# First chunk of a long convolution in two causal halves of 256 rows, so that the first FFN unit follows the first half

## The chip, the cores and the metric

One Trainium2 chip, one of its cores. The metric is the device time of one execution in microseconds, a median over executions. A profile adds the span, which is 1.7 to 1.8 us shorter than the time of the same execution (before: the profiled execution took 358.32 us, span 356.5).

## The reference, cut to what matters

Two layers, each a gated long convolution followed by a gated FFN, on 2048 rows of width 512 (FFN width 1792):

```python
def _A_ref(q, k, v, shift_k, ssm_k, ssm_D):
    k_shift = sum over t in 0..3 of k_pad[:, t:t+S, :] * shift_k[:, 3-t]   # cut: a loop
    kv = k_shift * v
    y = irfft(rfft(kv padded to 2S) * rfft(ssm_k padded to 2S))[:S]        # cut: causal convolution
    y = y + kv * ssm_D
    return q * y
def _B_ref(x, w_gate, w_up, w_down):
    return (silu(x @ w_gate) * (x @ w_up)) @ w_down

x = A_q
x = x + _A_ref(_layernorm(x), A_k, A_v, A_shift_k, A_ssm_k, A_ssm_D)
x = x + _B_ref(_layernorm(x), B_w_gate, B_w_up, B_w_down)
# and the same two lines once more
```

k, v, ssm_k are the same in both layers, so the convolution result y is computed once.

## The kernel before

The rows go in four chunks of 512. A chunk's y comes from products of spectra X (of k_shift * v) and G (of the filter h = ssm_k, D added to its row 0), each a 1024-point transform made by TensorE matmuls with tables `fwd` and `inv`, ScalarE evictions and VectorE butterflies. The FFN runs in 16 units of 256 rows (layer, chunk, half). A planner in the kernel's own Python gives each operation a cost and each transfer a latency (`lat`), and from these it works out one fixed order for each engine. TensorE, VectorE, ScalarE and the queue on SP each work through their order. Where the planner sees the head idle, it puts dummy matmuls (`wm`) to hold the clock.

The head, in program order (cut):

```python
transpose_k(0, "pf", ("ACT", "DVE"))               # k of chunk 0, 16 TensorE transposes
hs = transpose_h(0, "pf", (2, 0, 1, 3), False, ("ACT", "DVE"))
shift_mul(0, "pf", False)                          # 64 matmuls, then times v
normed[0, 0, 0] = apply_norm(0, 0)
...
for par in (0, 1):
    half(hs, ev, par, 2.0 / N, "pf", ("ACT", "ACT"), False)   # transform of h, 512 rows
    butterfly(ev, G[0], par, False)
...
direct(vt[0], X[0], "pf", ("ACT", "ACT"))          # transform of k_shift*v, 512 rows
for slot in (0, 2, 1, 3):
    product(0, 0, [slot], False)
...
inverse_direct(0, (0, 2, 1, 3))
first = prologue(0, 0, 0, True)                    # y -> x -> statistics -> z -> zT
prologue(0, 0, 1)
...
conv(1)
for c in range(NB):
    run((0, c, 0)); run((0, c, 1))                 # FFN units
    ...
```

The constants at the top say which engine does which statistics (`ST1`, `ST2`), normalisations (`Z_ACT`, `N_ACT`), h transposes (`H_DMA`) and residual adds (`X_PE`, an add by an identity matmul), and with how much slack the planner works (`SLK`, `ASL`, `HSL`). They were searched for this kernel.

## Time and profile before

| | before |
|---|---|
| time, median of 2 runs | 357.74 us (357.62 to 357.85) |
| span of the profiled run | 356.5 us |
| first FFN matmul | 37.09 us |
| TensorE work ahead of it, without dummies | 28.1 us |
| last matmul ends | 353.19 us |
| VectorE, ScalarE busy | 281.1, 238.0 us |

How to read it: split the span at the first FFN matmul and at the end of the last matmul. Ahead of the first cut TensorE has 28.1 us of work and 9.0 us without. Between the cuts lie 316.1 us; the counted work there is 342.5 - 28.1 = 314.4, so 1.7 us are waits. After the last matmul come 3.3 us. The 28.1 us are TensorE's busy time from 7.07 to 37.09; the count by pitch gives 27.8, so head idle and waits of the kernel before are good to some 0.3 us. And its profiled execution (358.32 us) is among the slowest on record for it: the run "fewer dummies in the kernel before" below has the same head and tail in an execution of 357.67 us, and its middle is 315.5 us, 0.6 less. So 1.1 us of waits are usual. I use the same four terms (head idle, waits in the middle, tail, work) for every kernel below, with work otherwise counted by matmuls and their pitch (the time from the start of one to the start of the next) and not by busy time.

### The profile page before, as it was taken

To read this page: it belongs to the slowest core of one execution; us is meant where nothing else is said; L and a number is where in the kernel's file an instruction comes from. 1 tells how busy PE (TensorE), PEld (TensorE's weight loads), DVE (VectorE), ACT (ScalarE), POOL (GpSimd) and SP (SyncE) were. 2 spreads that over 40 slices of the span, in tenths; PEclk is the share of its full clock that TensorE was granted. 3 is DMA by queue.
4 is the path that set the end of the run, shared out by engine and by line. 5 is a ranking of instruction groups with operands and counts; after the bars stand their busy time and mean duration, and the time that the engine had idled before them with its cause. 6 is when DMAs were issued, how large, how long until landed. Compare 5 with 4: busy or idle time off the path is not lost.

```text
span 356.5 us, 6735 instructions
## 1 busy us (share of the span) xinstructions
PE 347.6 (97%) x2689; PEld 254.4 (71%) x2712; DVE 281.1 (79%) x517; ACT 238.0 (67%) x454; POOL 39.3 (11%) x42
## 2 busy tenths in 40 slices
PE   7999999999999999999999999999999999999996
PEld 6655985867778585868668685858686777768673
DVE  6997999999989999999999999889985323626020
ACT  4587693838878493648878994848484775647352
POOL 1010010130320200111121000201101000101000
PEclk9999999999999999999999999999999999999999
DMA  7999021010241341010311042010103020101000
GB/s 263 306 353 293 2 69 22 0 31 2 45 119 45 63 147 31 0 31 1 79 40 31 1 116 63 2 29 3 31 29 31 30 31 1 31 1 31 30 2 29
DMA packets 37897, 21.98 MB, mean 62 GB/s; under 512 B 29797, under 2 KB 35690, under 8 KB 37866
## 3 DMA queue, kind: packets, MB, share of 16 engines
q1 hardware_dynamic: 37336, 21.03, 22.9%
q10 hardware_dynamic: 530, 0.53, 0.5%
q8 instruction: 21, 0.34, 0.4%
q14 instruction: 10, 0.08, 0.1%
HBM read 12.33 MB, written 2.10 MB: 40 GB/s over the span
## 4 chain that ended last, share of the span: by engine, by line
PE 49%; DVE 35%; ACT 10%; POOL 3%; issue 2%; DMA 1%; ACTq 0%; POOLq 0%; DVEq 0%
PE pf L335 30%; PE pd L851 15%; DVE m L518 4%; DVE ht L844 3%; DVE bnst L706 3%; DVE t L641 3%; DVE t L635 3%; DVE t L651 2%; POOL rstd L736 2%; ACT H L423 2%; DVE Z L656 2%; PE ps L335 2%; PE wm L1020 1%; DVE t L620 1%; DVE Z L648 1%
## 5 line engine op out<-in xcount | busy, mean ns | idle before, releaser
L335 PE MATMUL pf<-zT,wu_sb 128*128 128x256 bf16 x896 | 116.1, 273 | 0.1
L335 PE MATMUL pf<-zT,wg_sb 128*128 128x256 bf16 x896 | 116.1, 273 | 0.0
L335 PEld LDWEIGHTS <-wg_sb 128*128 128x128 bf16 x896 | 87.6, 98 | 18.9 <-issue 0.8
L851 PE MATMUL pd<-wd_sb,ht 128*128 128x512 bf16 x434 | 98.6, 380 | 1.5 <-DVE ht L844 0.8
L335 PEld LDWEIGHTS <-wu_sb 128*128 128x128 bf16 x896 | 87.6, 98 | 11.1
L837 ACT ACTIVATE sg<-pf 128x512 bf16<-128x512 f32 x112 | 68.9, 615 | 18.2 <-PE pf L335 16.7
L851 PEld LDWEIGHTS <-ht 128*128 128x128 bf16 x448 | 43.6, 98 | 49.8 <-DVE ht L844 1.2
L841 ACT CAST ht<-pf 128x512 bf16<-128x512 f32 x112 | 67.3, 601 | 15.0 <-PE pf L335 14.6
L844 DVE TENSOR_TENSOR ht<-ht,sg 128x1024 bf16<-128x1024 bf16 x64 | 39.5, 619 | 25.7 <-ACT ht L841 25.7
L711 POOL TENSOR_TENSOR rstd<-ve,nhalf 128x2 f32<-128x2 f32 x25 | 26.0, 1039 | 203.2 <-DVE ve L709 180.8
L706 DVE BATCH_NORM_STATS2 bnst<-xc 128x6 f32<-128x512 bf16 x50 | 32.5, 685 | 6.2 <-ACT xc L857 5.6
L863 ACT CAST dn<-pd 128x512 bf16<-128x512 f32 x24 | 12.9, 591 | 34.5 <-PE pd L851 34.5
L870 DVE TENSOR_TENSOR xc<-xc,dn 128x1024 bf16<-128x1024 bf16 x12 | 8.2, 686 | 17.8 <-ACT dn L863 17.8
L635 DVE TENSOR_TENSOR t<-X,G 128x2048 bf16<-128x2048 bf16 x18 | 21.9, 1219 | 0.0
L641 DVE TENSOR_TENSOR t<-X,G 128x2048 bf16<-128x2048 bf16 x18 | 21.9, 1217 | 0.0
L736 POOL TENSOR_TENSOR rstd<-ve,nhalf 128x2 f32<-128x2 f32 x7 | 12.0, 1719 | 80.0 <-DVE ve L732 80.0
L423 ACT ACTIVATE X<-ps 128x512 bf16<-128x512 f32 x32 | 18.8, 635 | 1.2 <-PE ps L335 1.1
L423 ACT ACTIVATE H<-ps 128x512 bf16<-128x512 f32 x24 | 13.4, 645 | 4.3 <-PE ps L335 4.3
L656 DVE TENSOR_TENSOR Z<-Z,t 128x2048 bf16<-128x2048 bf16 x12 | 14.7, 1222 | 0.1
L651 DVE TENSOR_TENSOR t<-t,t 128x2048 bf16<-128x2048 bf16 x12 | 14.6, 1221 | 0.1
L335 PE MATMUL ps<-vt,fwd 128*128 128x512 bf16 x54 | 14.4, 380 | 0.1
L335 PEld LDWEIGHTS <-fwd 128*128 128x128 bf16 x96 | 9.3, 98 | 7.2
(95 smaller groups left out, 316.5 us busy)
## 6 DMA issues: line engine op xcount, KB each, us to landing
vt<-in_A_v_dram SPq DMA_DIRECT2D x4, 512.0 KB, 4.6
xc<-in_A_q_dram SPq DMA_DIRECT2D x4, 512.0 KB, 4.8
out_dram<-xc SPq DMA_DIRECT2D x16, 128.0 KB, 1.7
wg_sb<-in_B_w_gate_dram SPq DMA_DIRECT2D x1, 1792.0 KB, 9.2
wu_sb<-in_B_w_up_dram SPq DMA_DIRECT2D x1, 1792.0 KB
wd_sb<-in_B_w_down_dram SPq DMA_DIRECT2D x1, 1792.0 KB, 12.3
hn<-in_A_ssm_k_dram SPq DMA_DIRECT2D x3, 512.0 KB, 7.6
hn<-in_A_ssm_k_dram ACTq DMA_DIRECT2D x1, 512.0 KB, 3.9
```

The costliest lines, as they stand in the source:

```text
L335: nc.tensor.matmul(o, lhsT=lhsT, rhs=rhs, start=(n == 0), stop=(n == len(terms) - 1))
L423: add("ACT", act(D), lambda: nc.scalar.activation(out=view(), in_=ps.t[:], func=ACT.Copy, scale=scale), r=[ps], w=[(buf, keys)], conv=conv)
L635: dve(n * D, lambda t1=t1, part=part: nc.vector.tensor_mul(out=t1.t[:], in0=x.t[:, sl, 0, :], in1=g.t[:, sl, part, :]), [(x, key(slots, (0 ...
L641: dve(n * D, lambda t2=t2, part=part: nc.vector.tensor_mul(out=t2.t[:], in0=x.t[:, sl, 1, :], in1=g.t[:, sl, 1 - part, :]), [(x, key(slots ...
L651: dve(n * D, lambda t1=t1, t2=t2, comb=comb: nc.vector.tensor_tensor(out=t1.t[:], in0=t1.t[:], in1=t2.t[:], op=comb), [t2], [t1], conv=conv)
L656: dve(n * D, lambda t1=t1, part=part: nc.vector.tensor_add(out=z.t[:, sl, part, :], in0=z.t[:, sl, part, :], in1=t1.t[:]), [t1], [zk], con ...
L706: add("DVE", 0.6, lambda st=st, i=i: nc.vector.bn_stats(out=st.t[:], in_=xs[c].t[:, i, :]), r=[(xs[c], (i,))], w=[st])
L711: add("POOL", PW, lambda: nc.gpsimd.tensor_tensor(out=rstd.t[:], in0=ve.t[:], in1=nhalf.t[:].to_broadcast((P, n)), op=ALU.pow), r=[ve, nha ...
L837: add("ACT", act(D), lambda ps=ps, o=o, sg=sg: nc.scalar.activation(out=sg.t[:, o:o + 2, :], in_=ps.t[:], func=ACT.Silu), r=[ps], w=[(sg, ...
L841: add("ACT", act(D), lambda ps=ps, o=o, ht=ht: nc.scalar.copy(out=ht.t[:, o:o + 2, :], in_=ps.t[:]), r=[ps], w=[(ht, (o // 2,))], due=(uni ...
L844: dve(n * W, lambda sg=sg, ht=ht: nc.vector.tensor_mul(out=ht.t[:], in0=ht.t[:], in1=sg.t[:]), [sg], [ht], due=(unit, k / pairs, 0.0, "h"))
L851: nc.tensor.matmul(pds[o].t[:], lhsT=ht.t[:, q, o * P:(o + 1) * P], rhs=wt["d"].t[:, ft, :], start=(ft == 0 and not xpe), stop=(ft == NF - 1))
```

## The change

Intent: the convolution is causal, so the first 256 rows of y need only the first 256 rows of k, v and h. The first FFN unit, which takes just these rows, can start when a half-size convolution is done, and the second half and block 1 fill TensorE behind it. For the later chunks the full 512-row spectra H0 and X0 are still needed. But the halves hold their rows two to a partition and the full form needs four, so eight re-layout transfers within SBUF (four for h, four for k_shift * v) turn one into the other. The weights come in 12 pieces. All searched constants changed with it.

The diff, cut to its core:

```diff
+    def half_block(h, view, buf, dst, scale, ring):       # transform of 256 rows
+        for q, ch in enumerate("ab"):
+            for part in (0, 1):
+                ...
+                add("PE", pe(2), ... r=[(buf, range(HP * h, HP * h + HP)), (fwd, (0, 1))], w=[ps])
+                evacuate(ps, dst, (2 * slot + part,), ..., scale, "ACT", False)
+    def relayout(src, skeys, dst, view):
+        m = P // 2
+        for h in range(HP):
+            for b in range(2):
+                add("SP", 0.6, lambda h=h, b=b: nc.sync.dma_start(
+                    out=view(dst)[m * h:m * h + m, 2 * b:2 * b + 2, :], in_=src()[b:P:2, HP * h:HP * h + HP, :]),
+                    r=[(skeys[0], skeys[1](h))], w=[(dst[0], dst[1](h, b))], lat=2.6, conv=True)
+    def load_weights(n, after=()):                        # 3 of 12 pieces
+        ...
-    wg = load_weights("g", -57)
-    load_weights("u", -56, after=[wg])
-    load_weights("d", -55, after=[wg])
+    last = load_weights(0)
+    for n in range(1, 4):
+        last = load_weights(n, last)
...
+    turn_k(0, "pf", ("ACT", "DVE"))
+    turn_h(0, "pf", ("ACT", "DVE"))
+    shift_half(0, "pf")
+    half_block(0, hrow, hsx, gh, 4.0 / N, "pf")
+    half_block(0, vrow, vt[0], xh, 1.0, "pf")
+    product_half(0, 0, True)
+    turn_k(1, "pf", ("ACT", "ACT"))
+    turn_h(1, "pf", ("ACT", "ACT"))
+    half_block(1, hrow, hsx, gh, 4.0 / N, "pf")
+    inverse_half(0, "pd")
+    first = prologue(0, 0, 0, True)                       # rows 0 to 255
+    shift_half(1, "pc")
+    ...                                                   # gh sums, two more products, second half
+    prologue(0, 0, 1)
+    relayout(lambda: hsx.t[:, 0], ..., hview, lambda d: hsx.t[:, 1])
+    H[0] = forward4(hsx, "H", 2.0 / N, "pc", True, lambda r: hsx.t[:, 1, r, :], ...)
+    relayout(lambda: vt[0].t[:], ..., vview, lambda d: kv4.t[:])
+    X[0] = butterfly4(forward4(kv4, "X0", 1.0, "pc", True, ...), True)
...
-H_DMA = lambda b: b in {2, 3}
+H_DMA = lambda b: b in ()
-X_PE = lambda l, c, h: (l, c, h) in {(0, 3, 1), (1, 1, 0), (1, 2, 0), (1, 3, 1)}
-SLK = 8.52
+SLK = 11.52
 (ST1, ST2, Z_ACT, N_ACT: other sets; ASL 8.04 to -4.88; HSL 13.4 to 28.72)
```

## The prediction

> **What bounds the kernel now.** I read the page first (engine shares, then the 40 slices), then the groups by shape of each engine, then busy time by stretch, then the timelines of the head and of the tail. The shares and the slices:
>
> ```profile
> PE 347.6 (97%) x2689; PEld 254.4 (71%) x2712; DVE 281.1 (79%) x517; ACT 238.0 (67%) x454; POOL 39.3 (11%) x42
> ...
> PE   7999999999999999999999999999999999999996
> ...
> DVE  6997999999989999999999999889985323626020
> ACT  4587693838878493648878994848484775647352
> ```
>
> TensorE (PE) is above 90% in every slice but the first and the last; VectorE (DVE) is nearly full in the first 30 slices (until about 270 us) and loose afterwards; ScalarE (ACT) always has room. The full PE row also covers the head, where the diff wants to gain. Busy time by stretch (columns: length, then busy time of PE, weight load, DVE, ACT, POOL; clock; DMA) says how full:
>
> ```profile
> 0.00:7.07 7.07, 5.24 (x50) 4.95 (x51) 4.07 (x15) 2.60 (x4) 1.31 (x10) 1.00 0.74 267
> 7.07:37.09 30.02, 28.14 (x235) 17.26 (x238) 27.30 (x61) 22.00 (x38) 2.56 (x3) 1.00 1.03 298
> 37.09:122.00 84.91, 84.06 (x692) 63.15 (x694) 80.87 (x143) 57.79 (x119) 13.72 (x8) 1.00 0.16 37
> 122.00:262.00 140.00, 139.25 (x1037) 102.05 (x1045) 135.00 (x224) 102.44 (x198) 15.61 (x13) 1.00 0.18 44
> 262.00:353.19 91.19, 90.88 (x681) 66.94 (x685) 33.85 (x78) 52.49 (x97) 6.12 (x8) 1.00 0.10 18
> ```
>
> The cuts are the first real PE work (7.07, transposes of k), the first FFN matmul (37.09), the end of DVE's work for the last convolution (262), and the end of the last matmul (353.19). Before 7.07 PE ran 5.0 us of dummy matmuls and 0.3 us of tap transposes. From 7.07 to 37.09 it idled only 1.9 us; the remaining 316 us have 1.9 us of idle in all. So the 37 us ahead of the first FFN unit are not lost: 28 of them are matmuls that must be done at some time. Lost are about 7 + 2 at the start, 2 later, and 3.3 after the last matmul: 14 us.
>
> Two timeline lines show the head's stop and the first FFN matmuls, and the last line is the tail (start, length, what):
>
> ```profile
> 8.85 0.39 PE L475 MATMUL pt<-ident,hn 128*128 128x128 bf16 x4 [0.73 <-ACT kTb L383]
> ...
> 37.09 1.03 PE L335 MATMUL pf<-zT,wg_sb 128*128 128x256 bf16 x8
> ...
> 352.80 1.07 ACT L857 CAST xc<-pd 128x512 bf16<-128x512 f32 x2 [3.30 <-PE pd L851]
> ```
>
> **What the Trainium skill says.** (1) "Perfetto Trace Analysis", section "Identifying the Most-Contended Engine": matmul busy time is no measure of nearness to roofline, since matmuls are pipelined. Agreed: a record of 128x256 averages 273 ns, yet eight take 0.875 us from start to start. So I count PE by pitch, not by record. (2) "TensorE: Matmul & The Clock Gate", "Wait — 56ns, not 53.3ns?": warm, start to start is N / 2.4 GHz plus about 2.5 ns. The trace agrees: 0.109 us for N = 256, 0.217 for N = 512, 0.056 for N = 128, at granted clock 1.00. (3) "VectorE: DVE Perf Modes", "The perf-mode tier table": tensor_tensor on bf16 in SBUF runs at 2x and falls to 1x with an operand in PSUM. The trace agrees: 1219 ns for 2048 elements, 425 against 687 ns for 512. (4) "DMA: Bandwidth & Descriptors", "Issuing engines are not separate DMA queues": splitting loads over SP and ACT adds no bandwidth. In the trace the head moves 263 to 353 GB/s.
>
> **PE work, part by part.** FFN: 16 units of 112 matmuls x 0.1093 and 28 x 0.2166 = 18.31 us, 292.9 in all. The change doesn't touch it. The rest before: X_PE 8 x 0.2166 = 1.7; transposes (k 16, h of blocks 0 and 1 32, tables 14, zT 8) 70 x 0.057 = 4.0, taps 0.3; shift matmuls 192 x 0.0557 = 10.7; forward transforms 96 x 0.2166 = 20.8 (h0 16, v0 32, 8 for each of six others); inverses 32 + 3 x 8 = 56 x 0.2166 = 12.1. Sum **342.5**; the page gives 347.6 - 5.3 of dummies and taps = 342.3, so the count holds.
>
> After: X_PE gone. Transposes: k0, h0, h1 16 each as before, h2 and h3 now on PE (H_DMA empty) 32, k1 16, tables 10, zT 8 = 114 x 0.057 = 6.5. Shift 10.7. Forward: four half blocks of 8 = 32, but H0 and X0 are made again in the 512-row form for the later products (16), and six others 48: 96, 20.8 as before. Inverses 16 + 24 = 40: 8.7. Sum **339.6**: 2.9 us less. That is the only lasting gain on the full engine.
>
> **The head's latency.** Block 0's loads are 256 KB pieces; before, the first 512 KB of k landed 4.7 us after issue. I estimate the first half of k at 4 to 5 us and first PE work about 2 us sooner than 7.07. But the shift needs the tap diagonals (4 DVE products, 2.5 us, before ready at 8.1) and the copies of k (1.3 us each), so it starts about 9 (10.8 before). Then: shift and multiply 2.5 us, four evictions of the h half and four of the v half on ACT at 0.6 (to about 14.5), two slots of products at 4.1 us before (2.05 each: last end at about 17.5), inverse and Y 1.5, multiply and add 1.5, and from there statistics, pow, normalise, transpose and copy as before about 5: FFN starts near **25 to 26**, 11 to 12 us sooner. PE has in that first chain only 24 transposes, 32 shift matmuls and 24 of 512: 1.4 + 1.8 + 5.2 plus 0.4 of tables = 8.8 us. The second half can fill with 6.2 us before its products (16 transposes, 32 shift matmuls, 16 of 512), and block 1 a little more. Each filler needs an ACT eviction: ACT has some 10 us in the first chain and 10 in the fillers, in 20 us. I count 16 to 17.5 us of real PE work before 25.5, so 8 to 9.5 us idle in the head, against 9 before. Starting FFN 11 us sooner is a re-ordering of PE work, worth about 0 to 1 us.
>
> **DVE.** Removed: four butterflies 2.7, products 8.2, copies and tables 2.2, other block-0 multiplies 0.5. Added: products of the halves 4.4 + 4.4 + 5.8, the sum of the h halves 1.4, butterflies of H0 and X0 at 5.5 each (2 x 1.22, 2 x 0.69, 4 x 0.42): 27.0. Moved to ACT: about three more early statistics pairs (1.4 each) and six normalise pairs (0.66 each): -8.2; X_PE gone adds 2.0 of adds before chunk 3. Net **+7 to 8 us** before the last convolution ends (262 now). DVE idled 12 us in its first 262, apart from 3 us at the very start, so it can swallow this, but then has next to no spare. ACT gains some 34 us (272 of 355), spread. Neither ends as the bound by its sum; both make small PE waits likelier. Weights in 12 pieces land at a like rate (9 MB in the head at about 350 GB/s is 26 us) and group 0 precedes the first unit.
>
> **Sum.** Span before 356.5. PE work -2.9; head idle -0.5; PE waits after the head +1 (2 us now); tail +0.5, as X_PE goes from the last unit and an add of 0.69 us comes ahead of its store. That is a span of 354.6, and the median time lies 1.2 above the span: 355.8. I take 1 us off, by choice and not by count, because all the scheduling constants were retuned with the change. **Prediction: 354.8 us.**
>
> **Rivals.** (a) The gain the diff intends: FFN starts 12 us sooner and the end moves with it, 346 or so. For it: every FFN unit does start sooner. Against: PE is full from 10.8 us on; deferred work comes back in the units. That needs the 14 us of losses to shrink below 10, with 3.3 of tail and at least 4 of first load. (b) DVE becomes the bound: +7.5 us against a margin of 9 us between its end at 262 and the last chunk's first unit at 279 (the prologue takes 8). If ACT or PSUM waits keep it idle as now, chunk 3 waits: 358 to 364. Against: DVE's spare is 12 us and the loads that it waited for are split. (c) The fillers don't fit: two convolution PSUM buffers and 1.36 us copies hold up PE in the head, dummy matmuls in their stead, and idle is 14 instead of 9: 359. (d) The second unit waits for its half (10 DVE products, DMA transposes, 20 us after the first half): 2 to 4 us, unless block 1 fills it: 357.
>
> **Range and chances.** From my sum, waits of 2 us fewer give 351, of 4 more give 359. So 350.8 to 359.2. Faster by 2% needs under 350.6, below the good end; slower means over 364.9, only rival (b) with (c). Chances 0.08, 0.86, 0.06.
>
> **What would show it.** Right: first FFN matmul near 25 us; real PE work (without dummies) near 339.6; head idle 8 to 10 us; inverse matmuls 40, forward still 96; DVE busy near 289, ACT near 270, DVE full to beyond 260. Wrong: if PE before the first FFN matmul idles under 6 us (gain larger, rival a), or over 12 (c); if PE shows waits of several us released by DVE ahead of chunks 1 to 3 (b); if real PE work isn't about 3 us less, the count is wrong.

## The result

| | before | after |
|---|---|---|
| time, median | 357.74 us | 376.01 us (376.01 to 376.02, 2 runs) |
| span | 356.5 | 374.3 |
| first FFN matmul | 37.09 | 39.50 |
| last matmul ends | 353.19 | 369.59 |
| VectorE, ScalarE busy | 281.1, 238.0 | 288.5, 264.7 |

The ratio is 1.051 (1.047 to 1.056): 5% **slower**, where the prediction said 0.8% faster and held 359.2 for the upper end.

The page of the kernel after, the rows that answer to those of before, and the granted clock:

```profile
PE 350.8 (94%) x2737; PEld 257.5 (69%) x2763; DVE 288.5 (77%) x531; ACT 264.7 (71%) x502; POOL 39.4 (11%) x43
...
PE   7953999999999999999999999999999999999994
...
DVE  4972797898999999999999999999988162625120
ACT  4672998994888968575798999584767363838461
...
PEclk9995999999999999999999999999999999999999
```

TensorE's row has a hole in slices 3 and 4 (18.7 to 37.4 us), and in slice 4 the clock falls too. VectorE is in the nineties without a break from about 94 to 271 us. Busy time by stretch, with the cuts of the prediction's table moved to this kernel's first FFN matmul and last matmul:

```profile
0.00:39.50 39.50, 26.01 (x242) 19.11 (x246) 23.26 (x59) 21.34 (x39) 3.33 (x13) 0.87 1.00 293
...
80.00:240.00 160.00, 155.99 (x1188) 112.92 (x1197) 156.82 (x257) 125.97 (x247) 20.64 (x15) 1.00 0.17 41
240.00:369.59 129.59, 129.12 (x971) 95.65 (x978) 73.61 (x150) 77.53 (x140) 11.62 (x12) 1.00 0.08 19
```

TensorE's timeline from 20 us on names the hole:

```profile
22.77 1.89 PE L336 MATMUL ps<-hsx,fwd 128*128 128x512 bf16 x8
34.06 1.01 PE L336 MATMUL ps<-hsx,fwd 128*128 128x512 bf16 x2 [9.40 <-DMA hsx<-hsx]
34.87 1.27 PE L1088 MATMUL wm<-ident 128*128 128x128 bf16 x10
...
37.65 0.78 PE L860 MATMUL ptz<-ident,z 128*128 128x128 bf16 x8 [0.22 <-issue]
...
39.50 1.03 PE L336 MATMUL pf<-zT,wg_sb 128*128 128x256 bf16 x8 [0.15 <-ACT zT L862]
```

At 24.66 us the next matmuls in TensorE's order are two of the full-length transform of h (H0). They read rows that a re-layout transfer (`hsx<-hsx`) has to move, and TensorE stands for 9.40 us. Behind them in the order stand the transposes of z (`ptz`) and the first FFN matmul, which do not need the transfer. The timeline of the other engines shows that z was ready long before, and when the transfers were issued:

```profile
25.17 2.57 SPq L510 DMA_DIRECT2D hsx<-hsx  x4
...
27.27 0.73 DVE L814 TENSOR_SCALAR z<-xc,mv,rstd 128x512 bf16<-128x512 bf16 x2
```

z was there at 28.0 us, but its transposes began at 37.65. The four transfers were issued at 25.17 us and after, behind 12 weight loads on the same queue, and landed 7.2 to 7.6 us after issue. The planner had reckoned with 2.6 us.

The stop also costs clock. By stretch (length, then PE, PEld, DVE, ACT, POOL; clock):

```profile
24.66:34.06 9.40, 0.00 (x1) 0.03 (x1) 5.72 (x14) 1.03 (x3) 0.81 (x1) 0.66 0.97 244
34.06:39.50 5.44, 5.06 (x28) 2.95 (x30) 1.36 (x3) 3.90 (x9) 0.00 (x0) 0.64 1.08 243
```

The granted clock averaged 0.66 in the stop and 0.64 in the 5.4 us after it. The Trainium skill says in "TensorE: Matmul & The Clock Gate", "What's actually happening", that after an idle window of about 3.4 us the array runs at half its clock; a mean of 0.66 over 9.40 us fits that (full clock for 3 us and half for 6.4 would give it, by estimate).

The tail of the kernel after (timeline):

```profile
369.19 1.07 ACT L911 CAST dn<-pd 128x512 bf16<-128x512 f32 x2 [5.03 <-PE pd L904]
370.30 0.69 DVE L918 TENSOR_TENSOR xc<-xc,dn 128x1024 bf16<-128x1024 bf16 x1 [5.68 <-ACT dn L911]
371.02 0.81 SPq L927 DMA_DIRECT2D out_dram<-xc  x2
```

Without X_PE, an add of 0.69 us stands between the last eviction and the store, where before the eviction went straight to the store. It also takes both rows in one instruction, so the first store waits for both evictions: it is issued 1.43 us after the end of the last matmul (371.02 - 369.59), against 0.22 before (353.41 - 353.19).

In the four terms (us of the span; work in the head after: 58 transposes, 64 shift matmuls, 34 + 8 of 512 columns = 16.0):

| | before | predicted | after | after - before |
|---|---|---|---|---|
| counted TensorE work | 342.5 | 339.6 | 339.6 | -2.9 |
| head idle | 9.0 | 8.5 | 23.5 | +14.5 |
| waits in the middle | 1.7 | 2.7 | 6.5 | +4.8 |
| tail | 3.3 | 3.8 | 4.7 | +1.4 |
| sum (span) | 356.5 | 354.6 | 374.3 | +17.8 |

Against the usual execution of the kernel before (waits 1.1), the waits are +5.4 and the sum is +18.4, which agrees with the 18.3 us between the medians.

The count of work is taken over from the prediction; the trace agrees with it in numbers of matmuls (96 forward, 40 inverse; in a trace with all records, 448 of 448 for the down projection). For the middle after: 369.59 - 39.50 = 330.1, less 339.6 - 16.0 = 323.6.

### The profile page after: what moved, and what is told of

It reads as the page before. It is cut to its first block, busy times and chain, and to the rows that moved or that the text cites. A ratio compares the mean times of both kernels' runs of the same rounds, so it can differ in the third digit from the quotient of the medians.

```text
span 374.3 us, 6917 instructions
## 1 busy us (share of the span) xinstructions
PE 350.8 (94%) x2737; PEld 257.5 (69%) x2763; DVE 288.5 (77%) x531; ACT 264.7 (71%) x502; POOL 39.4 (11%) x43
## 4 chain that ended last, share of the span: by engine, by line
DVE 51%; PE 30%; ACT 11%; issue 3%; DMA 2%; POOL 1%; SPq 0%; ACTq 0%; DVEq 0%; POOLq 0%
PE pf L336 16%; PE pd L904 10%; DVE ht L897 5%; DVE t L718 5%; DVE t L712 5%; DVE m L607 5%; DVE bnst L766 4%; DVE Z L733 3%; DVE t L728 3%; PE ps L336 2%; DMA hsx<-hsx 2%; PE wm L1088 2%; DVE xc L837 2%; DVE n L836 2%; DVE xc L918 2%
## 5 line engine op out<-in xcount | busy, mean ns | idle before, releaser
L911 ACT CAST dn<-pd 128x512 bf16<-128x512 f32 x32 | 17.4, 589 | 38.4 <-PE pd L904 36.6
L918 DVE TENSOR_TENSOR xc<-xc,dn 128x1024 bf16<-128x1024 bf16 x16 | 11.0, 687 | 31.7 <-ACT dn L911 31.7
L766 DVE BATCH_NORM_STATS2 bnst<-xc 128x6 f32<-128x512 bf16 x46 | 29.8, 684 | 0.6
L548 ACT ACTIVATE H<-ps 128x512 bf16<-128x512 f32 x32 | 18.6, 631 | 10.0 <-PE ps L336 10.0
L336 PEld LDWEIGHTS <-fwd 128*128 128x128 bf16 x96 | 9.3, 100 | 16.5 <-issue 10.9
L788 ACT ACTIVATE jk<-xc,nm 128x512 bf16<-128x512 bf16 x18 | 13.5, 748 | 3.6 <-DVE nm L784 3.6
L336 PE MATMUL ps<-hsx,fwd 128*128 128x512 bf16 x23 | 6.9, 399 | 9.5 <-DMA hsx<-hsx 9.4
L810 ACT ACTIVATE z<-xc,nmr,rstd 128x512 bf16<-128x512 bf16 x18 | 13.8, 817 | 2.4 <-DVE nmr L803 2.4
```

The lines of the kernel that those rows point to most:

```text
L336: nc.tensor.matmul(o, lhsT=lhsT, rhs=rhs, start=(n == 0), stop=(n == len(terms) - 1))
L548: add("ACT", act(D), lambda: nc.scalar.activation(out=view(), in_=ps.t[:], func=ACT.Copy, scale=scale), r=[ps], w=[(buf, keys)], conv=conv)
L766: add("DVE", 0.6, lambda st=st, i=i: nc.vector.bn_stats(out=st.t[:], in_=xs[c].t[:, i, :]), r=[(xs[c], (i,))], w=[st])
```

## The experiments

Seventeen kernels ran. **Theory A**: the stop on the re-layout transfers of h, in TensorE's fixed order, makes most of the loss. **Rivals**: (D) VectorE, fuller by 7 us, is the bound; (R) the retuned assignments make the loss, not the halves; (F) the filler work of the second half and block 1 holds up the first chain. In every group the kernel before ran on the same chip, at 357.6 to 357.8 us.

One thing differs between profiles of the halves without any edit. The first dummies start 107 ns apart, later ones 56 ns; the change came at about 7.3 us in the profile of the changed kernel, at 5.8 in that without the wait and at 5.3 in that with the transfers ahead of three groups. Real work stands behind the dummies, so the first shift matmul came at 10.00, 9.27 and 9.03 us. Up to 1.0 us of the difference between two first FFN times is therefore not the edit's.

### The stop

**No wait.** H0's transform reads the rows as they lie before the re-layout, so it need not wait. The order on all engines is the same. It was meant to give a wrong result; the difference stayed within the tolerance of the comparison, so "correct" means nothing here.

```diff
-    H[0] = forward4(hsx, "H", 2.0 / N, "pc", True, lambda r: hsx.t[:, 1, r, :], ...)
+    H[0] = forward4(hsx, "H", 2.0 / N, "pc", True, lambda r: hsx.t[:, 0, r, :], ...)
```

> The changed kernel with the full-length transform of h (H0) reading the rows before their re-layout, so that nothing waits for the re-layout DMAs; the DMAs still run, the order of every engine is the same; the result is wrong on purpose. Theory A (the PE stop of 9.4 us at 24.7 to 34.1 us on these DMAs, and the half clock and dummies that follow it, are the head's loss): first FFN matmul near 30 us instead of 39.5, time 9 to 13 us less, 363 to 367 us. Rival B (DVE and ACT, with 7 and 27 us more work, set the end later in the kernel): the first FFN matmul comes sooner as well, but the time falls by under 5 us, to 371 or more. In both: even with FFN starting some 7 us sooner than in the kernel before, it stays slower than the 357.7 of before, as PE was not idle there.

Measured: 365.69 us (365.43 to 367.1), ratio 1.023. First FFN matmul at 28.79 us. So the wait costs **10.3 us**, and the kernel without it is still 8 us slower than before, although its FFN starts 8.3 us sooner than before's.

**Transfers ahead of two weight groups.** Only the order on SP changes: the four transfers of h go in front of the last six weight loads.

```diff
+        seq, place, when = plan.order(PASSES)
+        late = [o for o in seq if o in weight_ops]       # groups 2 and 3
+        seq = [o for o in seq if o not in weight_ops]
+        at = max(seq.index(o) for o in moved) + 1        # moved: the four transfers
+        seq = seq[:at] + late + seq[at:]
```

> The changed kernel with only the order of the SP queue changed: the four re-layout DMAs of h are issued ahead of the last two of four weight groups; result right. If the DMAs were late because they were issued behind twelve weight loads (issued at 25.2, landed at 32 to 34 in the changed kernel): issue near 20, landing by 24 to 25, no PE stop over 1 us there, first FFN matmul near 30, the same time as the run without the wait within 2 us. If the landing time is set by the traffic alone and not by the place in the queue: landing 7 us after issue, near 27, half the gain. Rival B: under 5 us gained.

Measured: 367.92 us (367.09 to 369.05), ratio 1.028, correct. TensorE's timeline:

```profile
26.45 1.01 PE L336 MATMUL ps<-hsx,fwd 128*128 128x512 bf16 x2 [2.77 <-DMA hsx<-hsx]
...
31.47 0.71 PE L336 MATMUL pf<-zT,wg_sb 128*128 128x256 bf16 x5 [0.32 <-ACT zT L862]
```

The transfers were issued from 16.3 to 19.0 us on instead of 25.2 to 27.2. They still took 7.7 to 9.3 us to land, so the stop shrinks to 2.77 us and 8.1 us are gained. An earlier issue helps; the landing itself did not get shorter.

**Transfers ahead of three weight groups.** The same edit with groups 1 to 3 behind the transfers.

> The changed kernel with its four re-layout transfers of h ahead of three weight groups (it was two in the run that moved them first); the order on TensorE, VectorE, ScalarE and GpSimd is the changed kernel's. Theory A (the stop on TensorE is the landing of these transfers, and the landing is set by their place behind the weights in the queue): they land at about 20 to 22 us, the stop at the full-length transform of H0 is below 0.5 us, and the time is that of the run without the wait, 365 to 366.5 us. Rival B (the weights then come too late instead): the stop moves to the first FFN matmul or to the z transposes, which wait for a weight or a z transfer, and the time stays at 367.5 us or more. Rival C (moving bytes in front of the h projections' own inputs delays the products): Y of H0 ends over 1 us later than 22.7 us.

Measured: **366.05 us** (365.99 to 366.66), ratio 1.024 (1.022 to 1.025), correct. TensorE's timeline:

```profile
21.79 2.32 PE L336 MATMUL ps<-hsx,fwd 128*128 128x512 bf16 x10
...
26.76 0.72 PE L860 MATMUL ptz<-ident,z 128*128 128x128 bf16 x8 [0.43 <-DVE z L814]
...
28.55 1.03 PE L336 MATMUL pf<-zT,wg_sb 128*128 128x256 bf16 x8
```

The two matmuls of H0 now run with the eight before them in one group of ten, without a stop, and no weight comes too late. Theory A as expected: a correct kernel, the same order of computation, 10.0 us faster than the changed kernel. The transfers were issued from 10.6 to 19.0 us on and landed 2.9 to 9.7 us after issue (median 6.2). Whether the place in the queue or the traffic counts more is not separated, since this run holds the other loads back too.

**z transposes first.** H0's matmuls may not be placed before z is done, and the planner makes a new order.

```diff
-    H[0] = forward4(hsx, "H", 2.0 / N, "pc", True, lambda r: hsx.t[:, 1, r, :], ...)
+    H[0] = forward4(hsx, "H", 2.0 / N, "pc", True, lambda r: hsx.t[:, 1, r, :], ..., first)   # after=first
```

> The changed kernel with the H0 matmuls ordered behind the transposes that feed the first FFN unit, re-planned. In the new PE order one gate group and two other matmuls stand ahead of the first H0 matmul. Theory A: first FFN matmul near 30, then PE still stops for the re-layout until about 34, so some 3 of the 9.4 us are regained and the clock stays up: 367 to 372 us. Rival B: within 2 us of 376.

Measured: 372.45 us (369.56 to 372.94), ratio 1.041, correct. TensorE's timeline:

```profile
29.91 1.03 PE L336 MATMUL pf<-zT,wg_sb 128*128 128x256 bf16 x8 [0.31 <-ACT zT L862]
...
33.99 0.38 PE L336 MATMUL ps<-hsx,fwd 128*128 128x512 bf16 x1 [2.61 <-DMA hsx<-hsx]
```

The first FFN matmul comes at 29.91, 9.6 us sooner than in the changed kernel, and part of the stop comes back behind it (2.61 us). The profile is of the fastest of five executions (369.56 us, 6.5 below the changed kernel). The other four took 371.54 to 372.94 at a granted clock of 0.987 to 0.995, so the median falls by 3.6 only; what slowed them was not looked for.

**An honest latency for the planner.** The planner is told 14 us instead of 2.6 for the transfers.

```diff
-                    r=[...], w=[...], lat=2.6, conv=True)
+                    r=[...], w=[...], lat=14.0, conv=True)
```

> The changed kernel with only the planner's figure for the landing of the re-layout DMAs raised from 2.6 to 14 us, all orders planned again: nine gate and up groups stand ahead of the first H0 matmul. Theory A: no stop for the re-layout, first FFN matmul near 30, time as in the run without the wait, 362 to 367 us, if the new plan is otherwise as good. Rival B: 371 or more. If the prediction's PE count holds, the head still idles about 13 us (30 minus some 16 of work), 4 more than before, so it doesn't reach 357.7.

Measured: 376.66 us (376.33 to 376.98), ratio 1.053, correct. The first FFN matmul comes at 29.80, so the stop is gone, and **nothing is gained**. The waits of the middle rose: TensorE's idle there, by busy time, is 11.75 us against 5.3 in the changed kernel. VectorE lost time early (38.5 of 50.2 us busy from 29.8 to 80; in the run without the wait 45.3 of 51.2), and the clock from 120 to 200 us was 0.96. Why the new order is so bad was not tested. It shows that a re-plan is a change of its own, so the runs that keep the order are the ones to read.

### What the head still lacks

**Fillers short.** On the kernel without the wait, block 1's four k copies on ScalarE do an eighth of their columns, and two sums of half spectra on VectorE 64 of 512 (wrong, within the tolerance; order unchanged). A memset on GpSimd sets the part of k that the copies no longer write.

```diff
-            dst = lambda dt=dt: kT[1].t[:, dt, PADL:PADL + L].rearrange("d (p r) -> d r p", r=R)
+            dst = lambda dt=dt: kT[1].t[:, dt, PADL:PADL + 64].rearrange("d (p r) -> d r p", r=R)
-            out=gh.t[:, 2:4, part, :], in0=gh.t[:, 2:4, part, :], in1=gh.t[:, 0:2, 1 - part, :], op=op),
+            out=gh.t[:, 2:4, part, 0:64], in0=gh.t[:, 2:4, part, 0:64], in1=gh.t[:, 0:2, 1 - part, 0:64], op=op),
```

> The run without the re-layout wait, with fillers of the head cut short: the four ACT copies of block 1's k (1.36 us each; two stand ahead of the first half's Y on ACT) to an eighth, the two DVE sums of the h halves (0.68 each, they stand ahead of the first unit's z) to 64 columns; same order, wrong result on purpose, one POOL memset added. If the fillers on in-order engines are why the first unit's chain took to 28.8 and not to 25.5 as predicted: first FFN matmul 2 to 4 us sooner, and, if head idle is what counts, the time by as much: 362 to 364. If deferred DVE work sets the end, the FFN starts sooner and the time stays within 1 us of 365.7.

Measured: 364.39 us (363.86 to 364.58), ratio 1.019. First FFN matmul at 27.36, 1.4 us sooner, and 1.3 us gained. Its first shift matmul came 0.3 us sooner as well (8.97 against 9.27), so the fillers cut here cost about 1.1 us. Rival F is real, and small.

**Fewer dummies.** On the kernel with the transfers ahead of three groups, the first batch of 51 dummy matmuls is cut to 32.

```diff
                             n = int((start - t - 0.4) / 0.085)
+                            n = min(n, 32)
```

> The run before with the first batch of cold dummy matmuls cut from 51 to 32, so that the first real TensorE work can start about 2 us earlier if its inputs are there. Theory (the dummies of the head are on the path to the first FFN unit): first real matmul at about 5.4 instead of 7.4 us, first FFN matmul some 1 us sooner, time 0.5 to 1.5 us below the run before. Rival (ScalarE, busy without a break from 14 us, sets the head): first FFN matmul within 0.4 us, time within 0.5 us; or the clock is granted later and it is slower by 0.5 to 1 us.

Measured: 365.87 us (365.7 to 365.98), ratio 1.023, correct. The first real TensorE work starts at 5.58 instead of 6.24, and the first FFN matmul at 28.34 instead of 28.55. The time moved as the rival expected, but the trace gives another reason for it: with fewer dummies the 107 ns pitch lasted into the real work, so the first of k's first eight transposes began 0.48 us sooner, but the last only 0.18 us sooner (6.67 against 6.85 us). The shift matmuls came 0.22 us sooner (8.81 against 9.03), and that is all that reached the FFN. ScalarE is nevertheless the full engine in the rest of the head. The stretch from 20 us to the first FFN matmul, of the kernel with the transfers ahead of three groups (fifth column ACT):

```profile
20.00:28.55 8.55, 7.30 (x69) 4.37 (x66) 7.15 (x18) 8.55 (x18) 0.81 (x1) 1.00 0.98 307
```

ScalarE is busy for 8.55 of 8.55 us. All evictions of the spectra's halves are on it. Earlier, too, the first half's Y waits for it. In the same trace:

```profile
17.09 1.89 PE L498 MATMUL ps<-zh,inv 128*128 128x512 bf16 x8 [0.37 <-DVE zh L478]
...
18.24 2.61 ACT L411 COPY kTb<-pt 128x512 bf16<-128x512 bf16 x2
...
20.42 1.34 ACT L503 CAST Yk<-ps 128x512 bf16<-128x512 f32 x2
```

The inverse was done at 18.98 us, and its eviction began at 20.42, behind two copies of block 1's k.

**Fewer dummies in the kernel before.** Second batch 17 to 6.

```diff
+                            n = n if start < 5 else min(n, 6)
```

> The kernel before with its second batch of dummy matmuls cut from 17 to 6: k has landed at 5.9 us and the dummies end at 7.02 us. If the head of the kernel before is TensorE's own work in order, with nothing else behind it, the time falls by 0.5 to 1.1 us (356.6 to 357.3). If what follows waits for VectorE or ScalarE or for transfers, nothing changes within 0.3 us. If the clock falls for want of dummies, it is slower by 0.3 to 1 us.

Measured: 357.68 us, ratio 1.000 (0.998 to 1.002). k's transposes moved from 7.07 to 6.12 and the first FFN matmul from 37.09 to 37.08. Nothing gained: VectorE's copies of k still began at 8.05, right behind the tap products (5.64 to 8.14).

### The waits in the middle

**Less VectorE work early.** On the kernel without the wait, the butterflies of H0 and X0 work on 64 of 512 columns (order unchanged; wrong, within the tolerance).

```diff
+    cut['w'] = 64
     H[0] = forward4(...); G[0] = H[0] = butterfly4(H[0], True)
     ...
     X[0] = butterfly4(forward4(kv4, "X0", 1.0, "pc", True, ...), True)
+    cut['w'] = None
```

> The run without the re-layout wait, with the two added full-length butterflies of block 0 (H0 and X0, 16 DVE instructions, 10.7 us) done on 64 of 512 columns; same instructions in the same order on every engine, wrong result on purpose. DVE loses some 9 us of work between 29 and 80 us. If DVE is what makes PE wait in the middle (PE idles 5.9 us between the first FFN matmul and the last matmul, 1.9 in the kernel before): idle falls to 3 or less and the time to 360 to 363 from 365.7. If those waits come from ACT or from the order alone: within 1 us of 365.7.

Measured: 365.03 us (364.79 to 365.45), ratio 1.021. VectorE's busy time fell by 7.3 us (281.1 against 288.4), and that gave 0.7 us. But that work lay before 80 us, where VectorE is not full (45.3 of 51.2 us busy).

**Less ScalarE work.** 36 statistics passes on ScalarE on 64 of 512 columns (order unchanged, the scale factors adapted; wrong, relative error 0.124).

```diff
-                out=jk.t[:], in_=xs[c].t[:, i, :], func=ACT.Copy, ...
+                out=jk.t[:, 0:64], in_=xs[c].t[:, i, 0:64], func=ACT.Copy, ...
```

> The run without the re-layout wait, with the 36 ACT passes of the layer-norm statistics done on 64 of 512 columns; same instructions in the same order, wrong result on purpose. ACT loses some 12 to 14 us of 265. If ACT's added load is what makes PE wait in the middle: 5.9 us of PE idle fall to 3 or less and the time to 363 or less. If DVE is the one: within 1 us of 365.7, apart from one statistics pass that lies in the head.

Measured: 366.40 us (365.82 to 366.86), ratio 1.025, 0.7 us more than its base. The head began 0.6 us later in the profile (first shift matmul at 9.85 against 9.27); the middle is the same, 330.6 us against 330.7. So 10.8 us of ScalarE work less (254.1 busy against 264.9) shortened no wait there.

**Less VectorE work throughout.** On the kernel with the transfers ahead of three groups, all 46 statistics of VectorE work on 64 of 512 columns (order unchanged; wrong, relative error 0.307), and the same in the kernel before as a control (0.296).

```diff
-            add("DVE", 0.6, lambda st=st, i=i: nc.vector.bn_stats(out=st.t[:], in_=xs[c].t[:, i, :]), ...
+            add("DVE", 0.6, lambda st=st, i=i: nc.vector.bn_stats(out=st.t[:], in_=xs[c].t[:, i, 0:64]), ...
```

> The changed kernel with its re-layout transfers moved up by three weight groups, and every batch-norm statistic of VectorE on 64 of the 512 columns (wrong on purpose; the order on every engine is unchanged): 46 instructions of 685 ns become about 0.15 us each, some 24 us less of VectorE work, most of it between 80 and 240 us where VectorE is busy 39 to 39.6 of every 40 us. The middle (first FFN matmul to last matmul) of that kernel holds 330.9 us, of which 323.6 are counted TensorE work: 7.2 us are waits. Theory D (VectorE, full, is late with what TensorE waits for): the waits fall to 2 to 3.5 us and the time to 361 to 362.5. Rival L (single chains of latency and the order of the engines make them; the run that freed 9 us of VectorE work in the first 80 us gained 0.7): the waits stay at 6 us or more and the time falls by less than 1.2 us, the head's part of it included.

> The same cut in the kernel before, as a control (wrong on purpose, same order): its waits of the middle are 1 to 1.7 us. Both theories: hardly anything to gain, 356.5 to 357.7 us. If it gains over 2 us, the cut shortens the head or the tail by itself, and the run on the changed kernel has to be read with that subtracted.

Measured: 362.43 us (361.31 to 363.03), ratio 1.014, which is 3.6 us below the 366.05 of its base; the control 356.49 us, ratio 0.997, 1.2 us below before. By stretch, 80 to 240 us, first the kernel before (columns: length; PE, PEld, DVE, ACT, POOL):

```profile
80.00:240.00 160.00, 159.19 (x1194) 116.08 (x1203) 152.19 (x261) 119.17 (x234) 20.90 (x16) 1.00 0.20 47
```

then the changed kernel with the transfers ahead of three groups:

```profile
80.00:240.00 160.00, 156.66 (x1224) 115.44 (x1223) 157.65 (x259) 129.11 (x251) 22.08 (x16) 1.00 0.16 36
```

then the same with short statistics:

```profile
80.00:240.00 160.00, 158.10 (x1233) 117.63 (x1243) 153.51 (x266) 130.10 (x255) 21.54 (x16) 1.00 0.16 37
```

VectorE is busy 157.65 of 160 us with the halves against 152.19 before. With 153.51 TensorE's idle falls from 3.3 to 1.9 us. The waits of the middle by count: 354.61 - 28.02 = 326.6, less 323.6 = **3.0 us, against 7.1** in its base (359.30 - 28.55 = 330.7, less 323.6). The profiled run was the fastest of its four (361.31), so it shows the effect at its largest; by the medians 3.6 us go, 0.5 of them in the head. The control's middle shrank as well, to 314.3, which is its counted work within the error of the count: 1.2 us below the usual 315.5, as in its time. Read at a like load of VectorE (153.5 here, 152.2 in the kernel before), 3.0 stand against the usual 1.1, so 4.1 of the extra 6.0 us (7.1 less 1.1) go with the load. Read with the same cut in both and by the medians, 3.1 less 1.2, only some 2 go. Either way rival D holds for the middle, for some 2 to 4 of its 6.0 us: a full VectorE makes waits, not as one stop but as many small ones. The larger ones are listed, with what ended them (total us, times, longest), in the waits of the kernel with the transfers ahead of three groups,

```profile
PE pf L336 <- ACT sg L890: 0.9, 2, 0.5
PE pf L336 <- DMA zT<-z: 0.9, 1, 0.9
PE ps L336 <- DVE vt L588: 0.6, 1, 0.6
PE ps L336 <- DMA kv<-vt: 0.6, 1, 0.6
PE pd L904 <- DVE ht L897: 0.6, 3, 0.3
PE ps L336 <- ACT ks L587: 0.4, 1, 0.4
```

and of the same with short statistics:

```profile
PE pf L336 <- ACT sg L890: 0.8, 2, 0.5
PE ps L336 <- ACT ks L587: 0.4, 1, 0.4
PE pf L336 <- DMA zT<-z: 0.4, 1, 0.4
PE pf L336 <- ACT zT L862: 0.3, 1, 0.3
PE ps L336 <- DVE Z L613: 0.2, 1, 0.2
```

No line stands out. The order is the same in both, and with the short statistics the waits for VectorE's `vt` and `ht` and for the re-layout of `vt` are off the list and that for the transpose of z is halved; those for two ScalarE passes (`sg`, `ks`) stay, and two small ones are new. The chains behind them were not followed link by link.

### The retuned assignments

Five runs ask whether the constants alone make the loss (rival R).

In the kernel before, all of the new assignments (statistics, normalisation, h transposes, no X_PE), re-planned:

```diff
-H_DMA = lambda b: b in {2, 3}
+H_DMA = lambda b: b in ()
-X_PE = lambda l, c, h: (l, c, h) in {(0, 3, 1), (1, 1, 0), (1, 2, 0), (1, 3, 1)}
+X_PE = lambda l, c, h: False
 (and ST1, ST2, Z_ACT, N_ACT of the changed kernel)
```

> The kernel before, with only the changed kernel's engine assignments (no residual through PE, h of blocks 2 and 3 turned on PE, more statistics and normalising on ACT), its own first chunk and its own timing constants; result right. If the retuned constants cost time apart from the halves: over 361. If the loss lies in the halves: PE work +0.2 us, DVE some 6 us less, ACT 18 more: 356 to 360.

Measured: 368.34 us (367.65 to 369.66), ratio 1.031; the first FFN matmul at 41.97.

Only X_PE taken out of the kernel before:

> The kernel before without the residual through PE: PE work 1.7 us less, four adds of 0.69 us more on DVE, one of them ahead of the last store; only 18 to 30 instructions change place on an engine. From the tail of the changed kernel (4.7 us against 3.3) I expect tail +1.3, PE -1.7, waits +0.5: 357 to 359. Theory R would need more: over 360.

Measured: 359.43 us (359.08 to 359.86), ratio 1.005. This run settles the tail: from the last matmul to the end it takes 4.5 us, against 3.3 in the kernel before, with X_PE alone taken out and the plan made anew.

Only ST1, ST2, Z_ACT and N_ACT of the changed kernel in the kernel before:

> The kernel before with the changed kernel's sets for statistics and normalising on ACT only. The run with all assignments was 10.7 us slower than before. Theory R: this carries most of it, 363 to 368. Theory N (any new plan that wasn't searched for costs some us by small waits, whatever it moves): some 3 to 8 us, and the run with only the slack constants changed costs a like amount.

Measured: 371.25 us (370.08 to 372.54), ratio 1.038.

Only the slack constants of the changed kernel in the kernel before (SLK 11.52, ASL -4.88, HSL 28.72):

> The kernel before, same instructions on the same engines, with only three slack constants of its planner set to the changed kernel's (11.52, -4.88, 28.72), so that some instructions change place. Theory N: 2 to 8 us slower, 360 to 366. Theory R: within 1.5 us of 357.7, as no work is moved between engines.

Measured: 359.66 us (359.62 to 359.91), ratio 1.006. These constants alter no computation at all, only the order.

The other way round: before's assignments and X_PE put into the halves (on the run with two weight groups moved), re-planned:

> The changed kernel with the re-layouts issued first, and the kernel before's engine assignments put back (residual through PE in four units, h of blocks 2 and 3 turned by DMA, the earlier sets for ACT), planned again; result right; base is the relayout-first run, 367.9. If the assignments are what costs the rest (theory R): 358 to 362. If the loss beyond the re-layout wait is in the halves or in how well the plan is fitted (theory N): 366 or more.

Measured: 384.42 us (383.6 to 385.01), ratio 1.075, which is 16.5 us **slower** than its base.

Theory R expected 358 to 362 us of this last run, and it did not come. But neither set did well in the other's kernel, and each re-plan here moved the time up, by 2 to 17 us, which is enough to hide a gain. The planner's other constants (`DUR`, `STRETCH`, `T0`, `RINGS`), which changed with the kernel too, were left as they were in all five runs. So R is not supported, and not excluded either. Apart from the tail, these runs give no part of the 18.3 us. They say that a loss seen after a re-plan proves nothing about the thing edited.

## Why the prediction was wrong

**The claim that held.** "Starting FFN 11 us sooner is a re-ordering of PE work, worth about 0 to 1 us." The kernel with the transfers ahead of three groups starts its FFN 8.5 us sooner than before and takes 8.4 us longer, so the earlier start bought nothing that shows. The counts held too: 96 forward and 40 inverse matmuls, VectorE busy 288.5 (said: 289), ScalarE 264.7 (said: 272).

**The step that failed: "so 8 to 9.5 us idle in the head".** It measured 23.5. The work in it was right (16.0; said: 16 to 17.5), its end was not: the first FFN matmul came at 39.50 and not at "25 to 26". Two parts:

- 39.50 to 28.55, 10.9 us: the stop on the re-layout transfers of h (1.0 us of it is the later start of real work in that profile, 10.00 against 9.03 at the first shift matmul). The prediction counted H0's and X0's extra matmuls but never asked what they read, nor where they stand in TensorE's order. The transfers sit on the queue behind 12 weight loads, and what stands behind their readers on TensorE stops with them. Taking the wait away gave 10.3 us, issuing the transfers sooner 10.0.
- 28.55 to 25.5, 3 us: the fillers were taken as free beside the chain. In the trace with the transfers ahead of three groups the first half's products end at 18.0 (said: 17.5), and "inverse and Y 1.5" took 3.7, to 21.8: ScalarE, which carries the evictions of both, copied block 1's k first. The steps after it took 6.8 (said: 6.5). Cutting some of the fillers short gave about 1.1 us of the 3; the rest is this reading of the trace and no experiment.

**Waits in the middle, the term "+1".** It measured +4.8, and +5.4 in the kernel with the transfers ahead of three groups (+6.0 against the usual execution of before). The prediction saw VectorE's margin ("it can swallow this, but then has next to no spare") and kept the danger for rival (b), as one stop ahead of chunk 3. What came was, for some 2 to 4 us of it, the same cause in another form: many waits of under 1 us. Taking VectorE work away throughout brings the waits from 7.1 to 3.0 in the fastest execution; the same cut takes 1.2 from the kernel before too.

**Tail, "+0.5".** It measured +1.4. The 0.69 us add was foreseen, but not that it makes the first store wait for both evictions. With X_PE alone taken out of the kernel before, the tail is +1.2.

**The rivals.** (c), fillers that hold up PE, had the direction of the head with a third of its size and not its mechanism. (b) named VectorE, its 358 to 364 from the wrong event. No rival named a transfer, though the diff has eight new ones in the first chunk.

**The microsecond taken off by choice** because the constants were retuned was not earned. Retuning makes a plan fit; it does not tell by how much. Nor do time and span differ by 1.2 us: that took the median of one pair of executions and the span of another. In one and the same execution it is 1.8.

In sum: of 18.3 us, the stop makes 10.0 to 10.3, by the times (up to 1 us of this may be the later start of real work in the changed kernel). The other 8.4 are, in spans and against the usual execution of before, head idle +3.6, waits in the middle +6.0, tail +1.6, work -2.9. None of the correct kernels beats the kernel before; the best one with the halves in full is at 365.87. Open stay about 2 us in the head, the rest of the waits in the middle, and why re-plans cost what they do.

## What to carry to other kernels

On an engine that works in order, ask of every instruction ahead of the one you want early: what does it read, when was that transfer issued, and what stands before it in its queue? A transfer's latency in a plan has to come from a trace at the same load (here 7.4 us, not 2.6), and moving its issue in front of bulk loads that aren't needed yet can cure the stop without touching anything else. And ask what an earlier start is worth where the bound engine is already busy: here it bought nothing, and the extra work that it took went to VectorE, whose spare time had kept TensorE fed. Last, look at more than one execution: the profile of the kernel before was 0.6 us slower than usual, and those of the halves reached their first shift matmul up to 1 us apart.

## What the Trainium skill lacked or had wrong

- "DMA: Bandwidth & Descriptors", "Latency and other measured facts", speaks of a fixed cost of about 2 us, most of it the way to HBM, and has no landing time for a copy within SBUF under load. Here four such copies of 128 KB landed 7.2 to 7.6 us after issue while the weights were loading, and 2.9 to 9.7 us when issued before three of the four weight groups.
- The same page, "Issuing engines are not separate DMA queues", says that the time to initiate a transfer is usually small beside the transfer. With the queue backed up, the issue of one weight piece of 512 KB took SP up to 2.56 us in the changed kernel (median time from issue to landing 8.9 to 9.5 us), and 12 pieces held the re-layout transfers back until 25.17 us.
- "Perfetto Trace Analysis", "Identifying the Most-Contended Engine", warns that matmul busy time is no good measure of how close a kernel is to roofline. The runs add that it hides short waits too: in the kernel with the transfers ahead of three groups, busy time shows 4.6 us of idle in the middle, the count by pitch 7.1.
- No page of it says how far re-ordering alone moves a full kernel: the slack constants, which alter no computation, made 1.9 us.
